# A gated linear attention and a gated MLP on one core: the order of the steps, and the engine of the steps that have a choice, written anew behind the first tenth

## The chip, the core and the metric

The kernel runs on one core of a Trainium2 chip. A core has a tensor engine (PE, with its weight loads shown as PEld), a vector engine (DVE), a scalar engine (ACT), GpSimd (POOL) and SyncE (SP, which here only starts transfers). Each engine works through its own queue of instructions strictly in the order in which the program issued them and waits at semaphores for the others. The metric is the time of one execution on the device, in microseconds.

## The reference

```python
# attention: 4 batches, 8 heads, 768 steps, head dimension 48
mag = sqrt(a_re**2 + a_im**2)
scale = minimum(mag, 0.999) / (mag + 1e-6)
for t in range(768):                      # complex state S, 48 x 48 a head
    S = (a_re + 1j * a_im)[t] * scale[t] * S + k[t] v[t]^T
    y[t] = q[t] @ S.real
x = y, heads side by side                 # 4 x 768 x 384
# gated MLP
h = gelu(x @ w_in);  u, v = halves of h   # 512 columns each
v = layernorm(v) * g_ln
gated = u * (w_sg @ v + b_sg)             # w_sg 768 x 768, over time
out = x + gated @ w_out                   # 512 x 384
```

## The kernel before

The recurrence is done in chunks of 128 steps, 24 chunks in all (g = 0 to 23, 6 a batch). The gates' logarithms are summed along time, and q and k are multiplied by the exponentials of these sums and by the cosines and sines of the summed angles; a chunk is then products of matrices: `pa` (k by q, masked to `am`), `ps` (v by k, the chunk's part of the state S) and `py` (am by v, and S by q), whose result `yp` goes to DRAM and comes back as `x`. The MLP splits every f32 operand into a high and a low part in f32r and makes each product from three matmuls (`mm3`, L230): `pv` and `pu` for x by w_in, `pvs` for w_sg, `po` for w_out. The attention's own matmuls are plain f32.

The work is cut into Python generators, one chain of steps for each piece: `l` load gates, `m` load q and k, `g` logarithms (`logs`), `e` scaling (`scale`), `t`, `p`, `s` angles and their sines, `v` load v, `r` rotate, `z` transposes into heads, `a` a chunk's products (`attend`), `n` the MLP's v half with its layernorm, `x` its u half with the gelu, `y` the spatial product, w_out and the store, `w` splitting of weights, `h` and `k` range checks of gates and weights for a fallback that is not taken, `ok` the verdict on them, `f` constant products. A string, `ORDER`, names the chains one after the other; each name runs the next step of that chain (`:3` three steps), which puts its instructions at the end of their engines' queues. So the string alone sets the order on every engine. Marks behind a name choose the engine of a step that has a choice (`alt`):

- products and differences of two tiles (`ew`): VectorE, or GpSimd with one mark
- copies out of PSUM (`evac`, L205/L207): ScalarE, or VectorE with a mark
- high parts (`high`): ScalarE, GpSimd with one mark, VectorE with two
- masking of `pa` (`causes`): one VectorE operation (L659), or with one mark a ScalarE copy (L656) and a GpSimd product (L657)
- `stoke` (L225): none, one or three constant products of two constant tiles, written to a tile that the next real product overwrites; they only keep the tensor engine at work

`act` puts an ACT_TABLE_LOAD (L193) ahead of a function whose table is not the one loaded last: logarithm and exponential are one table, sine and arctangent another, gelu the third. Other places that the prediction names: L412 `im<-im,inv` in `logs`, L466 `k<-k,em` in `scale`, L522 `left<-csn` in the angles (`turns`), L691 `S<-S,dec` in `attend`, L273 to L279 the first steps of splitting w_out, L871 to L873 the verdict `pok` and `oki`, and L980, where every engine loads the verdict into a register (TENSOR_LOAD) for the branch at the end.

Of the kernel before, what the change touches and what calls it, by code (L numbers as in the profile page):

```python
# [39 lines left out]
e3' e3 n0_0' f z3:3 z3'' p3:2 p3'' p3 f z3:3 f:2 z3 a3:3 f:2 a3 s3:3 w12 e3 a3'' a3:4 n0_0' a3 r4'' r4 w5 w10 t4 p4 v5  # L40
w10:2' w4'' r5'' g4 n0_0:2 z4:6 n0_0:3 z4 r5'' a4 a4'' o0 z4 n0_0:2 g4 l5:2 a4:2 z5:2 w5 a4'' a4 z5' z5:2 m4 z5 g4 m4
z5:2 n0_2 w5 l7 g4 g5 w5 a5 a4:2 a4'' w11 a5' n0_2 a5 a5'' a5' w14 p4:2 e4 n0_0' n0_0'' a4 e4 o1 w11 n0_2'' n0_2 v7
n0_0 p4:2 w11'' p4 s4' a5:2 n0_3 w15 g5:2 e4 e4'' s4:2 r6 e4 r6:2 g5 n0_3 n0_3'' r6 t5 p5 r6'' r6 z6 g5 w15 n0_0'' g5
r6'' z7 n0_0' n0_0'' r6 n0_3'' w5 x0_3 w15 g5 n0_2 g5 n0_3 n0_2 x0_3:2 w15:2 a6 a6' f:10 p5 v6 n0_2 n0_3 x0_3 n0_2''
# [39 lines left out]
def tile_kernel(ctx: ExitStack, tc: tile.TileContext, t_q, t_k, t_re, t_im, u_q, u_k, u_re, u_im, t_v, v, q, k, f_re, f_im,  # L84
# [317 lines left out]

    def logs(n):

        re, im = (part(n, x) for x in ("re", "im"))
        new(n, "inv", "e")
        e = part(n, "inv")
        act(re, re, AF.Ln)
        yield
        act(e, re, AF.Exp, scale=-1.0)  # L410
        yield
        ew().tensor_mul(im, im, e)  # L412
        yield
        new(n, "l")
# [199 lines left out]
    def attend(g):  # L614
# [48 lines left out]
        for g2 in range(early):  # L663
# [390 lines left out]
```

## Time and profile before

| | |
|---|---|
| median of 3 runs | 436.95 us (436.94 to 437.4) |
| profiled execution, span | 434.6 us |
| its own time taken as | the median, 2.35 us above the span |
| PE busy | 421.3 us (97%) |
| DVE busy | 364.5 us (84%), 620 instructions |
| ACT busy | 275.2 us (63%), 378 instructions, 50 of them table loads |
| POOL busy | 150.7 us (35%) |
| longest idle stretches of PE after the start | 1.47, 1.33, 0.89, 0.77 us |

No separate time stands beside the profiled execution, so its span is set against the median. Busy times are sums over an engine's instructions, and matmuls overlap, so PE's 97% says that it is seldom idle, not that it could not be faster. A row of a timeline begins with the start and the duration; in brackets stands how long the engine was idle before it and whose result ended that.

### The profile page before, as it was taken

What the parts mean: (1) busy time and instruction counts of PE and PEld (TensorE: products, weight loads), DVE (VectorE), ACT (ScalarE), POOL (GpSimd) and SP (SyncE); (2) the same over time, 40 slices, a digit from 0 to 9 for tenths busy, and PEclk for the clock granted to TensorE, in tenths of its full rate; (3) what the DMA queues carried; (4) which work ended last, traced back from release to release, by engine and by line L of the source; (5) the groups of instructions that cost most, each with busy time, mean ns of one, the idle gap of its engine ahead of it and who ended that gap; (6) DMA issues with size and microseconds to landing.
All of it is one profiled execution on the core that took longest, in us unless ns stands there. A gap on an engine that the chain in (4) does not pass through costs nothing.

```text
span 434.6 us, 10107 instructions
## 1 busy us (share of the span) xinstructions
PE 421.3 (97%) x3958; PEld 383.6 (88%) x3958; DVE 364.5 (84%) x620; ACT 275.2 (63%) x378; POOL 150.7 (35%) x234
## 2 busy tenths in 40 slices
PE   7999899999999989999999999999999999999994
PEld 6667688788999989889998999989999998899994
DVE  5899899999999999898898999997898776757363
ACT  6999898886999886695666776776750113342010
POOL 7214356203334154446022416532321011326130
PEclk9999999999999999999999999999999999999999
DMA  7577868789478898697959789568947964554531
GB/s 244 176 205 196 268 168 278 223 241 277 149 196 259 243 299 263 208 273 212 271 141 299 217 241 252 168 193 226 320 120 230 330 193 163 187 181 166 157 116 59
DMA packets 78540, 93.54 MB, mean 215 GB/s; under 512 B 10516, under 2 KB 60438, under 8 KB 78488
## 3 DMA queue, kind: packets, MB, share of 16 engines
q1 hardware_dynamic: 78344, 92.65, 71.2%
q8 instruction: 32, 0.52, 0.5%
q10 hardware_dynamic: 144, 0.20, 0.1%
q14 instruction: 20, 0.16, 0.1%
HBM read 69.23 MB, written 23.60 MB: 214 GB/s over the span
## 4 chain that ended last, share of the span: by engine, by line
PE 43%; DVE 29%; issue 8%; POOL 7%; ACT 6%; DMA 4%; SPq 0%; DVEq 0%; POOLq 0%
PE pvs L230 10%; PE pu L230 6%; PE po L822 6%; PE pv L230 4%; PE pa L649 4%; PE py L700 2%; PE pv L225 2%; DVE am L659 2%; PE py L705 2%; DVE tg L838 2%; DVE im L510 2%; PE warm L225 2%; ACT L193 1%; PE ps L675 1%; ACT csn L194 1%
## 5 line engine op out<-in xcount | busy, mean ns | idle before, releaser
L230 PE MATMUL pvs<-wsgh,vh 128*128 128x384 f32 x192 | 65.9, 343 | 0.0
L230 PE MATMUL pvs<-wsgh,vl 128*128 128x384 f32 x192 | 65.3, 340 | 0.2
L193 ACT ACT_TABLE_LOAD x50 | 64.2, 1283 | 1.7 <-PEq L1039 0.9
L230 PE MATMUL pvs<-wsgl,vh 128*128 128x384 f32 x192 | 64.9, 338 | 0.0
L649 PE MATMUL pa<-Q,K 96*64 96x64 f32 (+1 forms) x768 | 41.0, 251 | 1.5 <-DVE am L659 1.5
L649 PEld LDWEIGHTS pa<-Q,K 96*64 96x64 f32 x768 | 36.7, 137 | 6.0 <-ACT ep L194 1.6
L700 PE MATMUL py<-am,vbuf 128*64 128x128 f32 x384 | 39.0, 276 | 2.8 <-DVE am L659 1.7
L230 PEld LDWEIGHTS pvs<-wsgh,vl 128*128 128x128 f32 x192 | 36.1, 188 | 1.4 <-DVE vl L219 0.8
L230 PEld LDWEIGHTS pvs<-wsgh,vh 128*128 128x128 f32 x192 | 36.1, 188 | 0.7 <-issue 0.4
L230 PEld LDWEIGHTS pvs<-wsgl,vh 128*128 128x128 f32 x192 | 36.1, 188 | 0.0
L822 PE MATMUL po<-gh,wouth 128*128 128x384 f32 x96 | 33.0, 344 | 0.8 <-DVE oki L873 0.8
L705 PE MATMUL py<-Q,S 96*48 96x128 f32 x320 | 33.7, 272 | 0.0
L822 PE MATMUL po<-gl,wouth 128*128 128x384 f32 x96 | 32.6, 340 | 0.3 <-DVE gl L219 0.2
L230 PE MATMUL pu<-xh,winh 128*128 128x384 f32 x96 | 32.9, 342 | 0.0
L230 PE MATMUL pu<-xh,winl 128*128 128x384 f32 x96 | 32.3, 337 | 0.0
L822 PE MATMUL po<-gh,woutl 128*128 128x384 f32 x96 | 32.3, 337 | 0.0
L230 PE MATMUL pu<-xl,winh 128*128 128x384 f32 x96 | 32.3, 336 | 0.0
L659 DVE TENSOR_TENSOR am<-pa,masks 128x512 f32<-128x512 f32 x44 | 29.5, 682 | 2.4 <-PE pa L649 2.1
L219 POOL TENSOR_TENSOR gl<-tg,gh 128x384 fp32r<-128x384 f32 x15 | 18.6, 1237 | 34.0 <-DVE gh L216 15.1
L700 PEld LDWEIGHTS py<-am,vbuf 128*64 128x64 f32 x384 | 25.5, 136 | 5.2 <-DVE am L659 3.1
L230 PE MATMUL pv<-winh,xh 128*128 128x512 f32 x72 | 29.4, 408 | 0.0
L194 ACT ACTIVATE vr<-pv 128x512 f32<-128x512 f32 x24 | 14.3, 599 | 22.7 <-PE pv L230 13.7
(286 smaller groups left out, 1125.2 us busy)
## 6 DMA issues: line engine op xcount, KB each, us to landing
vbuf<-in_t_v_dram SPq DMA_DIRECT2D x24, 288.0 KB, 3.9
K<-rk SPq DMA_DIRECT2D x18, 384.0 KB, 4.4
Q<-rq SPq DMA_DIRECT2D x18, 384.0 KB, 6.8
x<-xd SPq DMA_DIRECT2D x9, 576.0 KB, 5.6
xd<-yp SPq DMA_DIRECT2D x48, 96.0 KB, 3.5
gr<-in_f_im_dram SPq DMA_DIRECT2D x12, 384.0 KB, 5.3
gr<-in_f_re_dram SPq DMA_DIRECT2D x12, 384.0 KB, 3.9
out_dram<-x SPq DMA_DIRECT2D x23, 192.0 KB, 3.5
```

The lines of the kernel that those rows point to most:

```text
L193: nc.scalar.preload_act_table_set(SETS[t])
L194: nc.scalar.activation(out, in_, func, scale=scale, **kw)
L219: ew().tensor_tensor(out=l, in0=src, in1=h.bitcast(F32), op=ALU.subtract)
L225: nc.tensor.matmul(o, mask[:, 0:n], u_turn[:, 0:o.shape[1]], start=True, stop=True, skip_group_check=True)
L230: nc.tensor.matmul(o, w(i), x(i), start=(i == 0 and j == 0), stop=(i == n - 1 and j == 2))
L510: nc.vector.tensor_tensor_scan(out=im[:, kt, :], data0=im[:, kt, :], data1=im[:, kt, :], initial=run["left", b, c0][:, kt:kt + 1] if c0 el ...
L649: nc.tensor.matmul(pa[rows, hh, j:], K(h)[:, j:j + KB], Q(h)[:, j:], start=True, stop=True)
L659: nc.vector.tensor_tensor(out=pairs(am), in0=pairs(pa), in1=causal, op=ALU.mult)
L700: nc.tensor.matmul(py[64 * e:64 * e + 64, p_, :], Vy(h)[:, 0:64], ams[h // 4][:, h % 4, :], start=True, stop=c == 0)
L705: nc.tensor.matmul(py[64 * e:64 * e + D, p_, :], Sb[:, h, :], Q(h), start=False, stop=True)
L822: nc.tensor.matmul(po[d], w[:, f, ds], g[:, f, :], start=f == 0 and j == 0, stop=f == NF - 1 and j == 2)
L838: ew().tensor_mul(tg, us[f], tg)
```

## The change

The first three lines of `ORDER` stay (up to some 30 us of the run). Everything behind them is written anew: which step comes when, and the marks. Operations and buffers are the same. Three code edits only let a step fetch a tile later than before, so that steps can stand in another order.

```diff
 ORDER = """
 ...
-s1:2 a0 e1 w3 t2 w6' w6 r1:2'' l3:2 g2:5 e0 w3:2 o1 v1 p2 z1 z1'' w3 w3' z1 z1' m2:2 e2:2 p2' e2 g3 p2 a0 w4 g3:2 w3'
+s1:2 a0 e1 w3 t2 w6' w6 r1'' g2 r1'' g2 l3 e0 l3 w1'' g2 o0 p2 g2 p2' g2 w3:2 z1 v1 z1 w3 z1 g3 e1 p2 e2:2 f p2 z1' m2
 ...
-y3_0:2'' y3_0' y3_3 h22:2 x3_0 k5 k7:2 y3_0:2 k5 ok:2 y3_0 x3_0 y3_0:2 y3_0' y3_0'' y3_0:10
+y3_0:2 k0 h10 h21 y3_0'' y3_0' y3_0 f x3_0 y3_0 k0 h21 k8 x3_0 y3_0 y3_0'' y3_0' y3_0:8 y3_0' y3_0 k8 y3_3 ok y3_0:7
+ok y3_0
...
     def logs(n):
-        re, im = (part(n, x) for x in ("re", "im"))
+        re = part(n, "re")
...
+        im = part(n, "im")
         ew().tensor_mul(im, im, e)
...
     def scale(n):
-        q_, k_ = (U[n][x] for x in ("q", "k"))
...
-            ew().tensor_mul(at(k_, i), at(k_, i), at(em, i))
+            k_ = at(U[n]["k"], i)
+            ew().tensor_mul(k_, k_, at(em, i))
...
-            ew().tensor_mul(at(q_, i), at(q_, i), at(ep, i))
+            q_ = at(U[n]["q"], i)
+            ew().tensor_mul(q_, q_, at(ep, i))
...
-        Sb = run.get(("S", g - 1))
+        Sb = lambda: run["S", g - 1]
```

The lines of the kernel after are those of before plus 6 to 8. What changes in number, over the whole program: constant products 40 to 37. ACT: 373 to 402 instructions in the path that runs; table loads 50 to 65, `kt` copies 11 to 20, `yp` copies 11 to 14, `gh` casts 9 to 12, copies of `pa` 4 to 1. DVE: 620 to 595; `kt` copies 19 to 10, `yp` copies 13 to 10, S times dec 12 to 6, `vl` 19 to 15, `am` 44 to 47, `im` by inv 7 to 10. POOL: 239 to 247; S times dec 4 to 10, `vl` 5 to 9, `em` from k and csn 0 to 4, `am` 4 to 1, `im` by inv 4 to 1. On PE, the places where plain f32 and f32r matmuls follow each other with no transpose between them: f32 then f32r 15 to 11, f32r then f32 9 to 5; with transposes between them 35 to 25. Table loads that stand between the matmuls of 80 and of 220 us of the run before: 24 to 32.

Three places, with the order of one engine before and after.

PE at the end of the program, in the last `po` products. `po` is one tile of the result, `pok` the verdict of the range checks. Before:

```order
L822 MATMUL po_5308<-gh_5187,wouth_124 128x384
L822 MATMUL po_5308<-gl_5193,wouth_124 128x384
L822 MATMUL po_5308<-gh_5187,woutl_125 128x384
L871 MATMUL pok_5333<-ones_5331,ok1_5319 1x2
L980 TENSOR_LOAD oki_5335
L822 MATMUL po_5351<-gh_5187,wouth_124 128x384
L822 MATMUL po_5351<-gl_5193,wouth_124 128x384
```

After:

```order
L830 MATMUL po_5318<-gh_5225,woutl_125 128x384
L879 MATMUL pok_5372<-ones_5370,ok1_5358 1x2
L830 MATMUL po_5328<-gh_5225,wouth_124 128x384
L830 MATMUL po_5328<-gl_5228,wouth_124 128x384
L830 MATMUL po_5328<-gh_5225,woutl_125 128x384
L830 MATMUL po_5338<-gh_5225,wouth_124 128x384
L830 MATMUL po_5338<-gl_5228,wouth_124 128x384
L830 MATMUL po_5338<-gh_5225,woutl_125 128x384
L988 TENSOR_LOAD oki_5374
```

The load of the verdict has moved from in front of the `po` products to behind the last of them.

DVE around the small copy `left` of the angles that before runs at 158 us; `am` is a masked `pa`, for which `py` waits. Before:

```order
L688 TENSOR_TENSOR S<-ps,S 96x384
L838 TENSOR_TENSOR tg<-u__1764,tg 128x384
L659 TENSOR_TENSOR am<-pa_114,masks 128x512
L522 COPY left<-csn_2059 128x3
L659 TENSOR_TENSOR am<-pa_1397,masks 128x512
L205 COPY dec<-pd 96x16
```

After:

```order
L526 SCALAR_TENSOR_TENSOR csn_2066<-csn_2066,im_1387 128x768
L530 COPY left<-csn_2066 128x3
L419 TENSOR_TENSOR im_1928<-im_1928,inv_2001 128x768
L696 TENSOR_TENSOR S<-ps,S 96x384
L473 TENSOR_TENSOR k_2064<-k_2064,em_2094 128x768
L211 COPY kt<-pk 128x384
L559 TENSOR_SCALAR csn_2066<-csn_2066 128x768
L667 TENSOR_TENSOR am<-pa_114,masks 128x512
```

The copy stood directly ahead of an `am`; now five other operations stand between them, and the product k by em next to it has come from POOL to DVE.

ACT in the logarithms and gelus that before run from 120.9 to 132 us (`l`, `im`, `re`, `inv` are gates, `u` a gelu). Before:

```order
L193 ACT_TABLE_LOAD
L194 ACTIVATE l_1607<-l_1607,cols 128x768
L207 COPY yp<-py 128x512
L193 ACT_TABLE_LOAD
L194 ACTIVATE im_1502<-im_1502 128x768
L194 ACTIVATE gh<-tg 128x384
L193 ACT_TABLE_LOAD
L194 ACTIVATE re_1069<-re_1069 128x768
L194 ACTIVATE gh<-tg 128x384
L194 ACTIVATE inv_1504<-l_1607,cols 128x768
L193 ACT_TABLE_LOAD
L194 ACTIVATE u__1751<-pu 128x384
```

After:

```order
L199 ACT_TABLE_LOAD
L200 ACTIVATE u__1632<-pu 128x384
L200 ACTIVATE gh<-tg 128x384
L199 ACT_TABLE_LOAD
L200 ACTIVATE l_1616<-l_1616,cols 128x768
L199 ACT_TABLE_LOAD
L200 ACTIVATE im_1402<-im_1402 128x768
L200 ACTIVATE gh<-tg 128x384 x2
L199 ACT_TABLE_LOAD
L200 ACTIVATE inv_1409<-l_1616,cols 128x768
L199 ACT_TABLE_LOAD
L200 ACTIVATE u__1749<-pu 128x384
```

A gelu now stands alone between two gate functions, which makes five table loads of four.

## Rows read from the trace of the kernel before

**Rows 1.** The page: busy time, share of the span and instructions of each engine, and the granted clock of the tensor engine in 40 equal slices, in tenths.

```profile
PE 421.3 (97%) x3958; PEld 383.6 (88%) x3958; DVE 364.5 (84%) x620; ACT 275.2 (63%) x378; POOL 150.7 (35%) x234
...
PEclk9999999999999999999999999999999999999999
```

**Rows 2.** Busy time of each engine in five stretches of the run: length, then PE, PEld, DVE, ACT and POOL with their instructions, the granted clock of PE, the share of the DMA engines and GB/s.

```profile
30.00:80.00 50.00, 47.21 (x581) 37.51 (x580) 46.61 (x74) 44.53 (x68) 25.69 (x34) 1.00 0.77 231
80.00:160.00 80.00, 79.14 (x831) 74.27 (x825) 77.38 (x119) 70.15 (x90) 24.98 (x37) 1.00 0.80 233
160.00:220.00 60.00, 59.40 (x628) 54.70 (x629) 53.39 (x89) 42.40 (x56) 24.49 (x32) 1.00 0.81 237
220.00:330.00 110.00, 109.73 (x1107) 104.63 (x1103) 99.46 (x158) 71.84 (x91) 36.48 (x44) 1.00 0.77 226
330.00:434.60 104.60, 98.27 (x669) 93.38 (x667) 64.92 (x142) 21.03 (x39) 26.50 (x38) 1.00 0.55 174
```

**Rows 3.** What PE waited for, over the whole run: total in us, times, longest.

```profile
PE py L700 <- DVE am L659: 1.7, 2, 1.3
PE pa L649 <- DVE am L659: 1.5, 1, 1.5
PE py L700 <- POOL am L657: 0.9, 1, 0.9
PE po L822 <- DVE oki L873: 0.8, 1, 0.8
```

**Rows 4.** Timeline of PE in short stretches: start, duration, operation, idle before it.

```profile
52.72 0.74 PE L649 MATMUL pa<-Q,K 96*64 96x128 f32 x12 [1.47 <-DVE am L659]
...
66.65 0.48 PE L230 MATMUL pv<-winh,xh 128*128 128x512 f32 x1
66.97 0.39 PE L230 MATMUL pv<-winl,xh 128*128 128x512 f32 x1
...
83.74 8.80 PE L225 MATMUL pv<-u_turn,masks 128*128 128x256 f32 x40
...
105.87 0.39 PE L230 MATMUL pv<-winl,xh 128*128 128x512 f32 x1
106.10 0.40 PE L230 MATMUL pv<-winh,xl 128*128 128x512 f32 x1
106.43 0.78 PE L649 MATMUL pa<-Q,K 96*64 96x128 f32 x13
...
160.60 0.44 PE L700 MATMUL py<-am,vbuf 128*64 128x128 f32 x4 [1.33 <-DVE am L659]
...
161.09 0.39 PE L700 MATMUL py<-am,vbuf 128*64 128x128 f32 x4
161.31 0.39 PE L705 MATMUL py<-Q,S 96*48 96x128 f32 x4
161.63 0.44 PE L230 MATMUL pu<-xh,winh 128*128 128x384 f32 x1
161.91 0.34 PE L230 MATMUL pu<-xl,winh 128*128 128x384 f32 x1
162.09 0.34 PE L230 MATMUL pu<-xh,winl 128*128 128x384 f32 x1
...
424.44 0.41 PE L822 MATMUL po<-gh,wouth 128*128 128x384 f32 x1 [0.77 <-DVE oki L873]
```

**Rows 5.** Timeline of DVE at the stalls of 51 and 159 us.

```profile
48.33 0.36 DVE L273 TENSOR_SCALAR bits<-raw 128x384 int32<-128x384 int32 x1 [1.92 <-DMA raw<-in_moe_w_out_dram]
...
51.89 0.68 DVE L659 TENSOR_TENSOR am<-pa,masks 128x512 f32<-128x512 f32 x1
...
157.99 1.97 DVE L522 COPY left<-csn 128x3 f32<-128x3 f32 x1
159.87 0.68 DVE L659 TENSOR_TENSOR am<-pa,masks 128x512 f32<-128x512 f32 x1
```

**Rows 6.** Timeline of POOL at the stalls of 78 and 159 us.

```profile
77.92 1.27 POOL L657 TENSOR_TENSOR am<-am,masks 128x512 f32<-128x512 f32 x1
...
158.11 1.82 POOL L466 TENSOR_TENSOR k<-k,em 128x768 f32<-128x768 f32 x1
```

**Rows 7.** The tile `left`: durations in ns (minimum, median, maximum), first and last start.

```profile
L522 DVE COPY left<-csn x6: 154/164/2639, 84.2 to 263.0; 128x3 f32<-128x3 f32 x6
```

**Rows 8.** Timeline of ACT: a function (sine), a table load and the next function (logarithm).

```profile
144.80 0.85 ACT L194 ACTIVATE im<-im 128x768 f32<-128x768 f32 x1
145.66 1.28 ACT L193 ACT_TABLE_LOAD   x1
146.95 0.94 ACT L194 ACTIVATE l<-l,cols 128x768 f32<-128x768 f32 x1
```

**Rows 9.** Groups of instructions by line and shape: count, busy time, mean ns of one, idle before.

```profile
L193 ACT ACT_TABLE_LOAD x50 | 64.2, 1283 | 1.7 <-PEq L1039 0.9
...
L207 ACT COPY kt<-pk 128x384 f32<-128x384 f32 x11 | 5.2, 469 | 1.2 <-PE pk L631 1.2
...
L205 DVE COPY kt<-pk 128x384 f32<-128x384 f32 x19 | 10.2, 547 | 0.4 <-PE pk L631 0.2
...
L691 DVE TENSOR_TENSOR S<-S,dec 96x384 f32<-96x384 f32 x12 | 7.1, 592 | 0.3
...
L691 POOL TENSOR_TENSOR S<-S,dec 96x384 f32<-96x384 f32 x4 | 4.9, 1234 | 9.8 <-DVE S L688 9.8
```

More of the change, by code (lines that the diff above doesn't have):

```diff
@@ L40 @@
[L40 to L44, printed above, removed]
@@ new lines @@
+z1 a0 w4 w3' e2 g3 z1 m2 z1 w3' w7 a0 p2 g3 p2' f a0 z1' p2 e2' l4 a1 w1' a1'' e2 w4 e2 g3 a1 e2 g3 e2' f e2 a1 p2 w4
+a0 e2 a1'' t3 w7' s2 f a0 s2 a1 v2 w7'' l4 g3 w4 a1 s2 w9 g3 f g3 e2 r3 r2 g4 g3:2 p3 r2 r3 a1 z3 w12 g3 z3' e3 w2''
+w9' w12 w4' p3 z2:2 e3 w12 z2 w9 a1 z2:3 z3 z2 e3 a2 z2 v3 w12 m3 e3' g4 a2'' e3 p3 g4 a2 m3 e2 a2 z3 e3 z3 a2:2 w4''
+a2'' p3 w12 e3 a1 p3 g4 z3 e3'' w12' w8 e3 l7 w8 e3 n0_0 p3'' p3 g4 z3 a3 z3 a2 a3 a2 w5 g4 s3 a3:2 w8' n0_0' a3'' a3
+n0_0 a2 s3 a3:2 s3 w5 t4 n0_0 r4'' n0_0 a3 r5'' e3 r4 z4 p4 z4 n0_0:2 r5'' n0_0 l5 z4:3 w10 v4 z4:3 n0_0 a4 a4'' a4
@@ new lines @@
+w10:2' e3 l5 a4 g4 z5:2 w5:2 a4'' z5:2 a4 z5 g4 a3 v5 g5 n0_0 m4 z5 g4 z5 n0_2 w11 a4' z5 a5 g5 a4 x0_0 a5 p4 n0_2 a5
+a5'' n0_0' p4 a4 m4 a4 n0_2' w11 w11'' e4 p4:2 w14 a5 e4:2 a5 n0_2 p4 s4' s4 e4'' s4 g5 n0_0'' r6 g5 w5' a5 n0_0 n0_3
+w15 r6:3 e4 r6'' t5 g5 n0_3 v6 w5 n0_0'' g5 f r6 z6 n0_0 g5 n0_3'' r6'' z7 n0_3'' w15 p5 w15:2 n0_2 p5 r6 x0_3 n0_2
+w15 x0_3 p5 w15' z6 x0_3 p5 w14:2 f w14 p5 x0_3 l6 n0_2 x0_3 w14 n0_0'' n0_3 a6 w14 o1 n0_2 n0_2' z7 a6 n0_3 a6 a7' a7
+n0_3 n0_2' m5 v7 n0_3 l7 n0_3:2 l6 x0_3 a6 n0_3 g6 a6 x0_3 a7 e4 x0_0 g5 n0_3 s5 a7'' e4'' g6 m5 p5 a6 n0_3 a6 n0_3''
@@ new lines @@
+a6 n0_3' a6 n0_3' g5 a6 a7 n0_3'' n0_3' a6 n0_3' a6 a7'' a6' e5 a7 a7'' a7 n0_3'' e5'' a7 o1 n0_3 n0_3'' g6'' s5:2 a7'
+e5 a7 y0_3 g6 r8 y0_3 v9 a6 v8 e5 r8 g7 x0_3 y0_3:2 r8'' r8 e5 r8'' r8 y0_3' y0_3 r8 g6 y0_3 t6 y0_3' x0_0'' y0_3
+y0_3' y0_3:2 y0_3'' g6 p6 z8 y0_3 a7' g6 z9 y0_3:2 r8 y0_3 x0_0:2 l8 x0_0 p6 g6 x0_0 y0_3 a8 z8 m6 a9 a8:3 y0_3'' x0_0
+z9 m6 p6 y0_3:2 a9'' g6 p6:2 y0_3 a9 f s6'' a8 a8'' g7 a8:2 e6 a8 a9' s6 e6' g7 a8 e5 e5' y0_3 a7 a8' a8 s6 r10 a9 l8
+e6 v10 g7 a9 r10 a9 r10'' y0_3 e6'' a8' y0_3 e6 g7 r10 x0_0 a8 y0_0 y0_3 r10'' t7 g8 g7 y0_0 y0_3 p7 y0_0 p7 y0_0 y0_3
@@ new lines @@
+g7 a9 y0_0:2 p7 r10 g7:2 z10 r10' r10 y0_0 m7 p7 g8 x0_0 y0_0' a10:2 z10 l9 p7 e7 p7 g8 a10 a9 y0_0' a9 y0_3 m7 a9'
+e7:2 z11 e6 a10' a9 z11 n1_0 a10 a9 f s7' s7 e7' s7 y0_0' a10 r12 e6 a10 y0_0 a10'' x0_0 a10:2 a11 a9 r12 g8 r12' r12
+y0_0 a10 e7 g8 y0_0'' r12 v11 a10 r12 n1_0 a10 g8 y0_0 y0_0' g8 n1_0 f a11'' a11 z12 g8 t8 r12' y0_0 n1_0 l9 f a10
+a11'' e7 y0_0 a11 a12 g9:2 p8 r12 p8 z13 y0_0' p8 z12 n1_0 y0_0'' a11'' n1_0 a11 a12:3 p8 g9 m8 n1_0 p8 v12 n1_0:2 g8
+y0_0' n1_0:2 y0_0 g9:2 n1_0 y0_0 n1_3 y0_0 n1_0 y0_0 e8 e8'' p8 l10 e8 f y0_0 a12 m8 s8:2 a12'' n1_0' g9 n1_3:2'' s8
@@ new lines @@
+a12 n1_0'' n1_0' r14 e7'' n1_0'' a12'' z13 a12 a13 t9 l10 n1_0'' y0_0 r14 n1_0 y0_0 n1_3 r14:2 v13 n1_3 n1_0' n1_3
+n1_0 n1_3 a12 n1_3:2 n1_0' n1_3:2 a13 e8' x1_3 a13 n1_3 e8 a13 f g10 z14 a13 m9 a12 p9 g9 p9 a13 n1_3 a12' a13 a13''
+x1_3 a13 z15 a13 r14'' y0_0 a13'' p9 r14 e8 r14 a12 n1_3' a13 f n1_3 r14 a14' n1_3'' a14 n1_3'' v14 n1_3:2' n1_3'' g9
+x1_3:2 a13 n1_3:2 x1_3:2 g9 p9 y1_3:2 p9 y0_0 y1_3 l11 z14 x1_3 y1_3'' g10 e9 z15 y1_3 g10 s9 y1_3 e8' a15 y1_3 s9 a14
+y1_3' s9 a15 a14 g10 e9'' a15 a14:3 r16' a13 m9 v15 a14'' t10 a14:2 x1_0 y1_3' e9 r16 y1_3 a15 r16'' e9'' f p10 a14'
@@ new lines @@
+r18 y1_0' y1_0:2 x1_0 p11 y1_0 p11 y1_0' n2_0 g12 y1_0 e11 y1_0 n2_0 y1_0 a16 a17 n2_0 y1_0 y1_0'' p11 k2 n2_0 p11 v19
+y1_0 v18 n2_0:2 a18 a17 n2_0 g12 n2_3 a19' a18' n2_0 h9 n2_0:2 z18 y1_0 z19 s11 a19'' y1_0 n2_0 y1_0 e11 y1_0 s11 n2_0
+y1_0:2 s11 n2_0 y1_0 a18 y1_0 a18' h9 m11 h1 n2_0' a19 r20' h16 a18 p12 a18:3 e10:2 n2_0'' a18 a19 f a19 g12 y1_0
+a18:2 p12 n2_0 n2_3'' a19'' a19 k2 a19 r20 a18 n2_3 r20 e11 a18 e11'' a19:2 a19' n2_0 a19 n2_3:2 n2_0'' n2_3 h22 n2_0'
+n2_3 r20 z20 g12 n2_3:2 n2_0'' n2_3 e11 r20'' x2_3 a19 n2_3:3 v21 n2_3 x2_3:2 z21 x2_3 n2_3' x2_3 h1 x2_0 p12 n2_3''
@@ new lines @@
+n2_3' a20 a21 a20 x2_3 n2_3 r20 h16 m12 n2_3'' a20 v20 r20'' x2_3 n2_3'' n2_3 n2_3'' g12 x2_0 p12 x2_0'' k3 r20 y2_3:2
+p12 a21 a20 x2_3 y2_3 y2_3'' k12 e12 y2_3' y2_3 k9 x2_0 k3 y2_3:2 k12 s12 k9 k1 x2_0 h22 f s12 z21 e12 y2_3'' s12
+y2_3' x2_0 r22' x2_0 y2_3:2 y2_0 y2_3 y2_0 e12 y2_3'' y2_3' z20 h20 y2_3 k1 m12 h17 x2_0 r22 a21 y2_3 a20:2 r22' a20
+y2_3'' x2_0 a20 r22 a19 e11 e12' a20 z22 a21 h11 e11'' e12 a20 a21 a20'' a20 a21'' h20 h11 a21 r22 y2_3'' h6 a21
+y2_3'' r22 a20' a21:2 e12 a21' a21 a22' r22 a22:2 r22 h3 a20 y2_3:2 y2_0' z23 y2_3 z22 y2_3 f z23 y2_3:2 v22 y2_3:2 h3
@@ new lines @@
+y2_0' e12'' x2_0 h6' y2_0'' y2_0:2 y2_0'' a22' y2_0:3 a22:2 a21 a22 h17 y2_3 a22:2 h14 a22 a21 v23 y2_0 a22' x2_0
+y2_0' a23 a22 a23 a22 a23 a23'' y2_0 n3_0 a23 a22 a23' y2_0' h5 n3_0' h2 y2_0 n3_0 h14 a23 n3_0:2 h5 h15 y2_0 n3_3 h2'
+n3_0 y2_0 y2_0'' n3_0:4 y2_0 h15 n3_0 h8 n3_0 n3_3 y2_0 k7 k6 h7 y2_0:2 n3_0 y2_0 n3_0' n3_3 n3_0'' n3_0' k6 h12 n3_3
+h8 n3_0' y2_0 n3_3 n3_0'' n3_0 n3_3:2 k7 n3_3:2 n3_0:2' n3_3 n3_0 x3_3 y2_0 n3_3 y2_0 x3_3 h12 k4 n3_3:2 y2_0 n3_3'
+n3_3'' x3_3 n3_3 n3_3' x3_3 n3_3' k4 x3_3 n3_3' k11 x3_3 y2_0 h0 h7 n3_3' h4 n3_3'' x3_3 n3_3 y3_3:2 k11 y3_3'' k5
@@ L687, in attend @@
             else:
-                nc.vector.tensor_tensor(out=Sn, in0=ps[0:2 * D], in1=Sb, op=ALU.add)
+                nc.vector.tensor_tensor(out=Sn, in0=ps[0:2 * D], in1=Sb(), op=ALU.add)
                 yield
@@ L704, in attend @@
                     h = 2 * p_ + e
-                    nc.tensor.matmul(py[64 * e:64 * e + D, p_, :], Sb[:, h, :], Q(h),
+                    nc.tensor.matmul(py[64 * e:64 * e + D, p_, :], Sb()[:, h, :], Q(h),
                                      start=False, stop=True)
```

44 lines of the change are left out of this document (7 added, 37 removed).

## The prediction

> **What bounds the kernel now.** First the page: PE is busy 97% of the span and DVE, the next, 84%, while the granted clock stands at its higher level (2.4 GHz) in all forty slices [rows 1]. Whatever shortens the run must therefore take work off PE or close one of its few idle stretches; work on another engine counts only through these. Second, the table of five stretches, because an average over the run hides the tight places. From 30 to 80 us PE loses 2.79 of 50 us; DVE is busy for 46.61 of these (93%) and ACT for 44.53 (89%). From 80 to 160 us DVE is at 97% and ACT at 88%, and PE loses 0.86 of 80. From 160 to 220 ACT falls to 71% and PE loses 0.60, from 220 to 330 it loses 0.27 of 110 [rows 2]. Third, the waits of PE: nearly all are for `am` (1.7, 1.5 and 0.9 us) and for the verdict of the range checks (0.8) [rows 3]. Fourth, the timeline of PE at these waits gives each its place: 1.47 us before 52.72, 1.33 before 160.60, 0.77 before 424.44 [rows 4], and the 0.9 us for POOL's `am` [rows 3] end when it is there at 79.19 [rows 6].
>
> The profiled span is 434.6 us and the median 436.95. I take the 2.35 us between them as unchanged, sum on the span and add them at the end.
>
> **The change part by part.** Operations are the same, so there are six places where time can come or go.
>
> *The end of PE.* Today PE loads the verdict into its register in the middle of the `po` products and idles 0.77 us for it [rows 4]. Behind the change this load stands after the last `po`, where nothing on PE follows but the branch. The two transfers on SP now stand ahead of SP's own load, the additions of `x` on DVE ahead of DVE's; the last transfer, on ACT, stands behind ACT's load, but the verdict's matmul comes six matmuls before the end, so it should be there. I take -0.77, with -0.77 and 0 as ends.
>
> *The stall at 159 us.* DVE's copy `left`, 128 x 3, took 1.97 us [rows 5], against a median of 0.164 [rows 7]. It ran while POOL multiplied k by em from 158.11 to 159.93 [rows 6], and ended 0.03 us behind that product. `am` stood next in DVE's queue and started at 159.87; PE idled 1.33 us for it. In the new order that product is on DVE itself and five operations lie between the copy and the next `am`. I take -1.33; if another POOL operation of two operands falls on a copy with an `am` behind it, this is 0. By the Trainium skill, "SBUF — State Buffer", section "Who interferes with whom", VectorE and GpSimd share a pair of ports that one instruction can hold for its whole length, so that the other is blocked and not slowed. The 1.97 against 0.164 us agree with it. By that rule the change's six more S times dec and four more `vl` and `em` each on POOL speak against it, since they hold the ports more often; no row says how many of them would fall on something that PE waits for.
>
> *The stalls at 51 and 78 us.* In the first, DVE had waited 1.92 us for a piece of w_out [rows 5], and `am` came out late behind the work piled up. In the new order the first operation on w_out still stands only four operations ahead of an `am`. I take 0, with -1.47 as the other end. In the second, `am` went through ACT and POOL, and POOL's half alone took 1.27 us [rows 6] where DVE's whole one takes 0.68 [rows 5]. Three of the four `am` of this kind become DVE's. But DVE is 93% busy there, and what the path through POOL costs in length it saves in queueing. I take 0, with -0.9 as the other end.
>
> *Plain f32 beside f32r on PE.* From a `py` group to the first `pu`, 0.32 us pass where 0.22 is the pitch of such groups (161.09, 161.31, 161.63), and from the first `pu` to the next 0.28, where 0.18 follows [rows 4]. So a return from f32 costs some 0.10 + 0.10 = 0.20 us. In the other direction 106.10 to 106.43 is 0.33, where the interval before was 0.23: 0.10 us. Before, 15 x 0.20 + 9 x 0.10 = 3.9; after, 11 x 0.20 + 5 x 0.10 = 2.7. I take -1.2. Where transposes lie between, 66.65 to 66.97 is 0.32, not 0.23, so a return is 0.09 dearer there; there are ten fewer changes of this kind, five of them returns: 0 to -0.45, and I take 0, since the first transposes may pay it anyway.
>
> *Three constant products fewer.* Twenty steps took 8.80 us on PE, so one is 0.44 [rows 4] and three are 1.3. Two of the three stood before `pk` and one before `py` of the early chunks, in the first stretch of the table, where PE has idle time anyway and DVE is busiest but for the next [rows 2]. I take half, -0.6, with -1.3 and 0 as ends. That the clock would miss them is a rival, below.
>
> *The load moved between engines.* DVE loses work: nine `kt` copies at 0.547 and six S times dec at 0.592 are 8.5 us of its 364.5, and the rest of its changes about cancel. POOL takes the six at 1.234, 7.4 us, and has room (35%). ACT takes nine `kt` copies at 0.469 = 4.2, and above all 15 more table loads at 1.283 = 19.2 us [rows 9]. ACT has 160 us free over the run, but nearly all behind 220 us. Between 80 and 220 us lie eight more loads, 10.3 us, and with the copies perhaps 15 us of new work; ACT is busy for 70.15 + 42.40 = 112.6 of 140 us there (80%) and would come to 127 (91%). That is above the 89% of the stretch from 30 to 80, in which PE loses 5.6%, and above the 88% of the stretch from 80 to 160, in which it loses 1.1% [rows 2]. Which of the two it will resemble depends on DVE, which stays where it is or gets a little lighter in both. One row speaks for 1.1% and one for 5.6%. PE's present loss in these 140 us is 1.46. At 1.1% it would be 1.5, at 5.6% 7.8. So the cost is 0 to 6.3 us, and I take 1.9, a third of the way, because the row with DVE at 97% is the nearer in time and in kind.
>
> *Sum.* -0.77 - 1.33 - 1.2 - 0.6 + 1.9 = -2.0. The span becomes 432.6 and the time 432.6 + 2.35 = 435.0 us.
>
> **The rivals.**
>
> *A: ACT becomes the second bound from 80 to 220 us (slower).* The mechanism is one: an isolated gelu between two gate functions makes two table loads, ACT's queue runs late, and with it everything behind it in program order: `kt` copies (which hold `ps` and so S and `py`), exponentials em and ep (which hold k, q and the transposes). PE then waits where today it waits for nobody. For it speaks that the new order has five loads in the place of four within a dozen instructions, and ACT's 91%. Against it, that today only one wait of any size comes from ACT's side (by way of POOL's `am`, 0.9) [rows 3]. Price: +6.3 us at the loss of the first stretch; with the other gains, of which the stall at 159 us is already counted in the 1.46, -0.77 - 1.2 - 0.6 = -2.6, the span is 438.3 and the time 440.7. It decides from about half that price: at +3.2 the time is 437.6. In the trace a load takes 1.28 us and the next function starts 0.01 us later [rows 8]. The Trainium skill, "ScalarE: Activation LUTs", section "Step-by-step: what each stage is for", puts a change of table at about 2.7 us with the drain; the rows show no such drain, so the measured 1.28 decides. By the page's figure the 15 loads would be 40 us and this rival nearly sure.
>
> *B: the waits come back elsewhere (no change).* The new order closes two stalls and opens as many of the same kind, the constant products only become idle time, and ACT costs its 1.9: -0.77 - 1.2 + 1.9 = -0.1, so 434.5 and 436.9. For it: about 4 us of such stalls inside a run at 97% look like what a dense order leaves, and DVE stays at 93 to 97% up to 160 us [rows 2].
>
> *C: everything closes (faster still).* ACT costs nothing, and the stalls at 51 and 78 us go too: -0.77 - 1.33 - 1.2 - 1.3 - 0.45 - 1.47 - 0.9 = -7.4 at most, and about -5 with half of the last five terms: 429.6 and 432.
>
> *D: the clock falls.* With fewer constant products PE could be granted the lower level (1.2 GHz) for a while. Today the clock holds through idle stretches of 1.47 us [rows 1, 4], and after the change PE has as much work as before, so I hold this for nearly excluded.
>
> **How the numbers follow.** A measurement of this kernel tells about 0.2%, 0.9 us, from no change, so "same" is 436.1 to 437.8. The forecast (434.0 to 436.0) has 0.45, A 0.24 (437.8 to 441), B 0.18, C 0.11 (430 to 434), D 0.02. Faster: 0.45 + 0.11 and a little of B's edge, 0.57. Same: 0.18, from B and the lighter half of A's edge. Slower: 0.25. The range leaves out half of C and the upper part of A: 432.0 to 440.0.
>
> **What would show it.** In the profile after: no idle time of PE at the end for the verdict; no copy `left` of 2 us with `am` right behind it; PE's busy time lower by 1 to 2.5 us; 65 table loads, some 83 us of ACT; the stretch from 80 to 220 with ACT near 90% and PE's loss not above 3.5 us. The prediction is wrong if PE's waits have ACT's copies and exponentials in them with over 3 us in total (A), if the sum of PE's waits is as it was (B), or if the granted clock leaves its higher level (D).

## The result, and the profile after

| | before | after |
|---|---|---|
| median | 436.12 us (434.87 to 438.08, 19 runs) | 438.65 us (436.99 to 442.19, 19 runs) |
| after : before | | 1.007, interval 1.0049 to 1.009 |
| span of the profiled execution | 434.6 us | 436.5 us |

The change makes the kernel slower by 0.7% (the medians lie 2.5 us apart), where I had forecast 435.0 us and faster. The page of the kernel after, to be held against [rows 1]:

```profile
span 436.5 us, 10115 instructions
## 1 busy us (share of the span) xinstructions
PE 419.2 (96%) x3952; PEld 382.7 (88%) x3952; DVE 357.2 (82%) x596; ACT 297.6 (68%) x406; POOL 169.7 (39%) x242
```

PE has 2.1 us less work, as forecast, and the run is longer: PE waits more. Its waits, to be held against [rows 3] (total, times, longest):

```profile
PE pa L657 <- DVE am L667: 2.9, 2, 2.3
...
PE py L708 <- DVE am L667: 1.2, 2, 0.9
PE pv L236 <- DVE xl L225: 1.1, 2, 0.7
PE pa L657 <- ACT Q L213: 0.8, 1, 0.8
PE phi L539 <- ACT im L200: 0.7, 1, 0.7
PE pk L639 <- DMA K<-rk: 0.6, 1, 0.6
PE pvs L236 <- POOL vl L225: 0.5, 1, 0.5
```

The wait for the verdict is gone and the number of waits has grown, but one stands out, 2.3 us for an `am`. The five stretches (busy time of PE, PEld, DVE, ACT, POOL, then the granted clock), to be held against [rows 2]:

```profile
30.00:80.00 50.00, 46.28 (x580) 37.02 (x580) 48.58 (x73) 44.87 (x71) 28.82 (x28) 1.00 0.77 229
80.00:160.00 80.00, 78.72 (x788) 74.06 (x783) 76.33 (x117) 70.70 (x89) 33.16 (x40) 1.00 0.79 235
160.00:220.00 60.00, 57.66 (x579) 52.25 (x578) 53.71 (x81) 52.31 (x69) 26.05 (x34) 1.00 0.83 238
220.00:330.00 110.00, 108.46 (x1097) 103.54 (x1094) 89.67 (x148) 82.23 (x105) 39.65 (x47) 1.00 0.77 226
```

PE's loss grows by 0.93, 0.42, 1.74 and 1.27 us. From 80 to 220 us ACT is busy for 123.0 of 140 us (88%, against 80%), near the 91% of my estimate, so this looks like rival A. And PE's waits for ACT (`Q`, `im` and two smaller ones) come to 2.1 us, where before has none of 0.2 us or more. The timelines at the two places that cost most say something else. First PE itself:

```profile
61.88 0.89 PE L657 MATMUL pa<-Q,K 96*64 96x128 f32 x16 [2.27 <-DVE am L667]
...
165.15 0.89 PE L657 MATMUL pa<-Q,K 96*64 96x128 f32 x16 [0.62 <-DVE am L667]
...
167.84 0.44 PE L708 MATMUL py<-am,vbuf 128*64 128x128 f32 x4 [0.92 <-DVE am L667]
```

Then DVE (start, duration) ahead of these waits:

```profile
57.44 0.54 DVE L473 TENSOR_TENSOR k<-k,em 128x384 f32<-128x384 f32 x1
57.91 2.16 DVE L478 TENSOR_TENSOR q<-q,ep 128x384 f32<-128x384 f32 x1
...
61.04 0.68 DVE L667 TENSOR_TENSOR am<-pa,masks 128x512 f32<-128x512 f32 x1
...
161.02 3.48 DVE L559 TENSOR_SCALAR csn<-csn 128x768 int32<-128x768 int32 x1
164.42 0.68 DVE L667 TENSOR_TENSOR am<-pa,masks 128x512 f32<-128x512 f32 x1
```

and POOL at the same times:

```profile
56.73 2.92 POOL L225 TENSOR_TENSOR wsgl<-raw,wsgh 128x768 fp32r<-128x768 f32 x1 [1.76 <-ACT wsgh L200]
...
159.84 1.47 POOL L699 TENSOR_TENSOR S<-S,dec 96x384 f32<-96x384 f32 x1 [0.18 <-DVE S L696]
161.28 1.84 POOL L478 TENSOR_TENSOR q<-q,ep 128x768 f32<-128x768 f32 x1
163.09 0.99 POOL L225 TENSOR_TENSOR gl<-tg,gh 128x384 fp32r<-128x384 f32 x1
```

The product `q<-q,ep` takes 2.16 us, where its equal in size just ahead took 0.54; it ends 0.4 us behind POOL's low part of w_sg. The copy `csn` (L559, the sign cleared ahead of the sines) takes 3.48 us; the median of its six is 0.546. It overlaps three operations of POOL that follow one another and ends 0.4 us behind the last. `am` stands behind both in DVE's queue. The mechanism looks like that of the stall at 159 us before [rows 5 to 7], which the change removed; this profile shows two others.

### The profile page after: what moved, and what is told of

It reads as the page before. It is cut to its first block, busy times and chain, and to the rows that moved or that the text cites. A ratio compares the mean times of both kernels' runs of the same rounds, so it can differ in the third digit from the quotient of the medians.

```text
span 436.5 us, 10115 instructions
## 1 busy us (share of the span) xinstructions
PE 419.2 (96%) x3952; PEld 382.7 (88%) x3952; DVE 357.2 (82%) x596; ACT 297.6 (68%) x406; POOL 169.7 (39%) x242
## 4 chain that ended last, share of the span: by engine, by line
PE 39%; DVE 8%; DMA 5%; ACT 3%; issue 2%; POOL 2%; SPq 2%; DVEq 0%; POOLq 0%; ACTq 0%
PE pvs L236 12%; PE po L830 7%; PE pv L236 7%; PE pu L236 6%; PE pa L657 3%; DMA xd<-yp 2%; DMA Q<-rq 2%; PE ps L683 2%; PE py L708 1%; DMA K<-rk 1%; DVE csn L559 1%; SPq L596 1%; PE py L713 1%; DVE lo L449 1%; ACT L199 1%
## 5 line engine op out<-in xcount | busy, mean ns | idle before, releaser
L199 ACT ACT_TABLE_LOAD x65 | 83.4, 1283 | 1.9 <-PEq L1047 0.9
L657 PE MATMUL pa<-Q,K 96*64 96x128 f32 (+1 forms) x768 | 40.8, 250 | 4.2 <-DVE am L667 2.9
L667 DVE TENSOR_TENSOR am<-pa,masks 128x512 f32<-128x512 f32 x47 | 31.9, 683 | 7.0 <-PE pa L657 6.7
L225 POOL TENSOR_TENSOR gl<-tg,gh 128x384 fp32r<-128x384 f32 x15 | 17.7, 1179 | 39.1 <-DVE gh L222 23.2
L236 PE MATMUL pv<-winh,xl 128*128 128x512 f32 x72 | 28.7, 398 | 1.2 <-DVE xl L225 1.1
```

Source lines behind the costliest of these rows:

```text
L199: nc.scalar.preload_act_table_set(SETS[t])
L225: ew().tensor_tensor(out=l, in0=src, in1=h.bitcast(F32), op=ALU.subtract)
L236: nc.tensor.matmul(o, w(i), x(i), start=(i == 0 and j == 0), stop=(i == n - 1 and j == 2))
L657: nc.tensor.matmul(pa[rows, hh, j:], K(h)[:, j:j + KB], Q(h)[:, j:], start=True, stop=True)
L667: nc.vector.tensor_tensor(out=pairs(am), in0=pairs(pa), in1=causal, op=ALU.mult)
```

## The experiments

Two theories. **Ports:** the loss comes from operations of VectorE held beside GpSimd just ahead of what PE waits for. **ACT:** it comes from 15 more table loads. Names such as `s7'` in the diffs are entries of `ORDER`; each ratio is to the kernel before, with its interval.

**No table loads.** `before_oneset` and `after_oneset` leave gelu, sine and arctangent out:

```diff
     def act(out, in_, func, bias=None, scale=1.0, **kw):
+        if table["on"] and table_of.get(func, 0):
+            func = AF.Identity
```

> The kernel before, with gelu, sine and arctangent replaced by the identity (these values are left out of the result), so that one table serves the whole run and 49 of 50 table loads go. Theory ACT (the change loses by its 15 more table loads): PE waits little for ACT today, so 0.993 to 0.998 of before. Theory ports (it loses where VectorE is held up beside GpSimd): 0.997 to 1.000.

> The kernel after with the same identity in place of gelu, sine and arctangent, so that 64 of 65 table loads go. Theory ACT: with the loads gone the shorter work of PE shows, 1.5 to 2.5 us below the same kernel made from before. Theory ports: it stays at least 1.5 us above that one.

Measured: 1.0055 (1.0035 to 1.0074) from before, 1.0097 (1.0062 to 1.0132) from after. Without its table loads after is not faster than before without them, so theory ACT, which wanted 1.5 to 2.5 us less, falls. (Part of the 0.4% between them is clock, below: 4 of the 6 executions of the second.) In its profile PE's waits for ACT have shrunk to 0.2 us and others stand in their place, 1.9 us for an `am` and 1.4 us for POOL's `vl` among them. Nor did ports foresee that before would become slower by 0.55% with ACT 64 us lighter. One new stall, in the timeline of DVE without loads:

```profile
134.83 3.37 DVE L444 TENSOR_TENSOR_SCAN lo<-going,lo 128x384 f32<-128x384 f32 x2
138.13 0.53 DVE L207 COPY kt<-pk 128x384 f32<-128x384 f32 x1
138.57 1.27 DVE L661 TENSOR_TENSOR am<-pa,masks 128x512 f32<-128x512 f32 x2
```

```profile
135.00 2.38 POOL L414 TENSOR_TENSOR im<-im,inv 128x768 f32<-128x768 f32 x1 [3.40 <-ACT inv L196]
```

The same two scans and the same product in before:

```profile
134.92 1.80 DVE L442 TENSOR_TENSOR_SCAN lo<-going,lo 128x384 f32<-128x384 f32 x2
```

```profile
136.26 2.10 POOL L412 TENSOR_TENSOR im<-im,inv 128x768 f32<-128x768 f32 x1 [4.57 <-ACT inv L194]
```

The scans take 3.37 us, not 1.80, while POOL has the product, which ACT released 1.3 us earlier than in before; PE waits 1.38 us for `am`. In this profile a lighter ACT moved work of POOL onto work of DVE.

**The two held operations**, first both, then one at a time:

```diff
-f s7' s7 e7' s7 y0_0'
+f s7:2 e7' s7 y0_0'
...
-a3:2 w8' n0_0' a3'' a3
+a3:2 w8 n0_0' a3'' a3
```

> The kernel after with two steps moved to other engines: the copy with the sign cleared ahead of the sines at 161 us from VectorE to ScalarE, and one low part of w_sg at 57 us from GpSimd to VectorE. Theory ports: the waits of PE of 0.62, 0.92 and 0.57 us from 164 to 178 go and that of 2.27 at 60 us shrinks to about 1.6, so 2 to 3 us less than after, 0.999 to 1.002 of before. Theory ACT: ScalarE gets 0.84 us more, so as after, 1.005 to 1.009.

> The kernel after with only the copy with the sign cleared (161 us) moved from VectorE to ScalarE. Theory ports: PE's waits of 0.62 and 0.92 us behind the held copy go, and the later load of K behind them, 1.5 to 2.1 us less than after, 1.002 to 1.004 of before. Rival (the gain of the two edits came from shifts all along the run): as after, 1.006 or more.

> The kernel after with only the one low part of w_sg (57 us) moved from GpSimd to VectorE. Theory ports: the wait of 2.27 us shrinks and part of it comes back 2 us later because VectorE has 0.95 us more to do, 0.7 us less than after, 1.004 to 1.007 of before. Rival: 1.007 or more.

Measured: both 0.9991 (0.9963 to 1.0019), `s7` alone 1.0043 (1.002 to 1.0066), `w8` alone 1.002 (0.9992 to 1.0048). From 1.007, that is 0.8%, 0.3% and 0.5%. With both, the loss of the change is gone; `w8` alone takes most of it; the 0.3% of `s7` lies within the two intervals, so it is not shown by itself. In `w8` alone the product of q by ep is short again (DVE's timeline):

```profile
56.50 0.55 DVE L477 TENSOR_TENSOR q<-q,ep 128x384 f32<-128x384 f32 x1
```

This repeats: in all four profiles that leave the low part of w_sg on GpSimd at that place (after, after without table loads, `s7` alone, and the kernel with S times dec on VectorE, below) the product takes 2.16 to 2.18 us, and in all six that move it in after's order 0.54 or 0.55.

The copy `csn` at 161 us does not repeat. In `w8` alone it is where after has it, with the same operations of POOL around it (DVE, then POOL):

```profile
158.98 0.71 DVE L558 TENSOR_SCALAR csn<-csn 128x768 int32<-128x768 int32 x1
```

```profile
159.24 2.17 POOL L477 TENSOR_TENSOR q<-q,ep 128x768 f32<-128x768 f32 x1
```

Here the copy ran through between two operations of POOL, and POOL's second took 2.17 us, not 1.84; PE waits for no `am` there, only 0.60 us for the transfer of Q. In after without table loads the same copy takes 0.72 us. So 3.48 us is what one execution shows, and the share of this copy in the loss stays open.

`w8` gave 2.2 us where I expected 0.7. Its wait of 2.27 us became one of 1.10 (the work now ahead of the next `am`), and the waits behind the copy were absent from its profile; the clock, below, may have a part.

**The same mechanism in before:** the stall mended, and the copy of the signs put on VectorE.

```diff
-s7 e7' p7 g8 a10 a10''
+s7 e7' g8 a10 a10'' p7
...
-a5'
+a5
```

> The kernel before with the small copy left at 158 us put behind the masked product that PE waits for, and with the masked product of 78 us made by one VectorE operation in place of ScalarE and GpSimd. If a stall of PE counts with its full width, 1.33 and up to 0.9 us go, 0.995 to 0.998 of before. Rival: what stands behind comes no earlier (transfers, other waits), 0.999 to 1.001.

```diff
-s7 e7' p7
+s7' e7' p7
```

> The kernel before with the copy with the sign cleared of the same angles moved the other way, from ScalarE to VectorE, where GpSimd's product of k by em runs beside it at 158 us. Theory ports: it is held until that product ends, and the masked product behind it comes later by 0.5 to 1.5 us, 1.001 to 1.004 of before. Rival: ScalarE has 0.84 us less to do and nothing is lost, 0.998 to 1.000.

Measured: 0.9985 (0.9964 to 1.0006) and 1.0019 (1.0000 to 1.0039). In the second the copy is held as expected:

```profile
158.92 2.36 DVE L551 TENSOR_SCALAR csn<-csn 128x768 int32<-128x768 int32 x1
161.20 0.16 DVE L522 COPY left<-csn 128x3 f32<-128x3 f32 x1
161.27 0.68 DVE L659 TENSOR_TENSOR am<-pa,masks 128x512 f32<-128x512 f32 x1
```

It ends at 161.28, 0.4 us behind a product k by em on POOL (159.05 to 160.86), and PE waits 1.81 us there. In the first, the wait at 159 us is gone from the profile, and at 78 us PE now waits 1.49 us for another `am`: a mended wait is worth less than its width.

**The end.** In before, the verdict placed as in after:

```diff
-ok:2
...
-y3_0:10
+y3_0:2 ok y3_0:7 ok y3_0
```

> The kernel before with the verdict of the range checks taken after the first of the last three results and loaded at the very end, as after has it. By the term of the prediction 0.77 us less, 0.998. Rival: the end is set by the additions and the store behind it, and nothing is gained, 1.000.

Measured: 1.0002 (0.9983 to 1.0022). PE's last matmul ends at 428.76 us, not 429.38, but the span is 434.8, not 434.6. The transfers of the last microseconds, KB and us from issue to landing, of before and then of this kernel:

```profile
out_dram<-x ACTq DMA_DIRECT2D x1, 192.0 KB, 3.0
```

```profile
out_dram<-x ACTq DMA_DIRECT2D x1, 192.0 KB, 3.8
```

The last store is issued 0.62 us earlier and lands 0.8 us slower; the two on SP ahead of it are slower too (3.0 us, not 2.2). Over the profiles of all kernels here, the time from PE's last matmul to the end of the span is 5.1 to 5.4 us in the seven with the early verdict, 5.5 to 6.1 in the thirteen with the late one (5.44 and 5.45 where they come nearest). Why the stores land slower stays open.

**Less work for GpSimd in general:**

```diff
-                ew().tensor_tensor(out=Sn, in0=Sn, in1=by, op=ALU.mult)
+                nc.vector.tensor_tensor(out=Sn, in0=Sn, in1=by, op=ALU.mult)
```

> The kernel after with all ten products S times dec on VectorE, none on GpSimd (before has four there). If it is GpSimd's use of the port in general, VectorE is held less and the run is 1 to 3 us shorter than after, 1.000 to 1.005 of before. If only the few places count where a held operation stands ahead of what PE waits for, VectorE's 5.9 us more are about as dear as what they save, 1.005 to 1.009.

Measured: 1.0076 (1.0054 to 1.0098), as after. At 57 us the product q by ep is held as in after (2.17 us), and PE waits 2.28 us. At 161 us the copy `csn` has no operation of POOL beside it and takes 0.55 us, but PE waits there all the same, for a transfer (DVE, then PE):

```profile
164.86 0.55 DVE L558 TENSOR_SCALAR csn<-csn 128x768 int32<-128x768 int32 x1
```

```profile
163.00 1.56 PE L656 MATMUL pa<-Q,K 96*64 96x128 f32 x32 [1.45 <-DMA Q<-rq]
```

So ten operations fewer on GpSimd left the hold at 57 us, and the time, as they were. This profile shows the clock. PE behind the wait at 60 us in after and then here, 62 to 66 us:

```profile
62.00:66.00 4.00, 4.00 (x54) 3.42 (x54) 3.77 (x7) 3.95 (x6) 0.00 (x0) 1.00 0.57 171
```

```profile
62.00:66.00 4.00, 4.00 (x48) 3.88 (x45) 3.42 (x7) 3.97 (x5) 0.00 (x0) 0.57 0.55 180
```

Behind a wait of the same length the granted clock stayed at its higher level in one execution and averaged 0.57 in the other, mostly at the lower level (1.2 GHz). Among all executions 8 of 19 of after have a mean granted clock under 0.995, 6 of 12 with `s7` mended, 8 of 11 here; with `w8` mended 1 of 12, and of before, as timed beside the experiments, 2 of 138. So the wait at 57 to 62 us comes with a lower clock in nearly half of the executions. It is not the only place that can: with the copy of the signs on VectorE in before (PE waits of 2.0 and 1.8 us) it is 4 of 12. What the fall costs is not settled by the record: in after the medians of the executions at 0.995 or more and of those below lie 0.5% and 0.8% above before, with `s7` mended 0.1% and 0.7%.

**More places mended, and orders joined.** After with `s7`, `w8` behind both `am`, and the low part of v at 117 us on VectorE; then two orders that join before and after and have this last edit too.

```diff
-f s7' s7 e7' s7 y0_0'
+f s7:2 e7' s7 y0_0'
...
-a3:2 w8' n0_0' a3'' a3 n0_0 a2 s3 a3:2
+a3:2 n0_0' a3'' a3 n0_0 a2 s3 a3 w8 a3
...
-n0_3'
+n0_3
```

> The kernel after with the copy with the sign cleared (161 us) on ScalarE, the low part of w_sg (57 us) on VectorE behind both masked products that PE waits for there, and the low part of v that PE waits for at 117 us on VectorE. Theory ports: all three of the waits behind held operations go (2.27, 0.62, 0.92, 0.55 us and the K load of 0.57), 4 to 4.9 us less than after, 0.995 to 0.999 of before. Rival: the waits come back at the next tight place, 1.000 to 1.003.

> The order of before up to some 65 us (372 steps), then the remaining steps in the order of after, with the sign copy at 161 us on ScalarE and the low part of v at 117 us on VectorE. Theory ports (the place at 57 us is avoided, the others are mended): idle time of PE about 1.5 us less than before and its work about 1 us less, the end 0.5 us longer, 0.994 to 0.998. Rival: the junction or other waits cost as much, 1.000 or more.

> The order of after with the three steps mended up to some 165 us (760 steps), then the remaining steps in the order of before, whose PE hardly waits there and which keeps its early verdict. Sum of the waits seen so far: about 2 us less idle time and 1.5 us less work than before, 0.991 to 0.996. Rival: the junction or other waits cost as much, 1.000 or more.

Measured: 1.0123 (1.0084 to 1.0162), 1.009 (1.0054 to 1.0125), 1.0177 (1.0144 to 1.0209), all slower. The edit at 117 us made a wait of its own (DVE, then PE, of the first):

```profile
111.72 0.69 DVE L224 TENSOR_TENSOR vl<-vr,vh 128x512 fp32r<-128x512 f32 x1 [2.23 <-POOL vh L219]
112.33 0.68 DVE L666 TENSOR_TENSOR am<-pa,masks 128x512 f32<-128x512 f32 x1
```

```profile
113.07 0.69 PE L707 MATMUL py<-am,vbuf 128*64 128x128 f32 x4 [2.39 <-DVE am L666]
```

```profile
113.00:117.00 4.00, 3.93 (x34) 3.60 (x35) 4.00 (x8) 3.94 (x5) 1.38 (x1) 0.57 0.00 0
```

VectorE's queue stands for 2.23 us for the high part, which GpSimd still makes, with `am` behind it; the clock falls behind the wait in the profiles of all three. Without this edit:

> The kernel after with the sign copy (161 us) on ScalarE and the low part of w_sg (57 us) on VectorE, behind both masked products that PE waits for there; the low part of v at 117 us stays where after has it. If the two held operations and the 1.1 us that the first form of the edit left are the loss: 0.995 to 0.999 of before, and the clock stays up. If there is more of the same elsewhere: 1.000 to 1.004.

> The order of before for 372 steps (some 65 us), then that of after, with only the sign copy moved to ScalarE; no new wait of VectorE for GpSimd's high part of v. Ports: without that 2.4 us wait and the fall of the clock behind it, 0.996 to 1.000. Rival: the later stretches of after are dearer than those of before whatever happens at 57 and 161 us, 1.003 or more.

Measured: 0.9985 (0.9962 to 1.0008) and 0.9994 (0.9963 to 1.0025), no execution under 0.995 in clock. The low part of v alone thus costs 1.4% (1.0123 against 0.9985), more than the wait of 2.4 us and the clock behind it; but the profile of the first shows the fastest of its six executions. That rest, and a wait of 3.07 us at 176 us in the third (for an `am` whose queue waited for ACT), were not followed up.

The first of the two kernels without the edit at 117 us also shows why the mended change brings no gain. In its profile PE has 2.4 us less work than in before (418.9 us, not 421.3) and as much more idle time, in waits of 1.0 us and less for VectorE, ACT and transfers.

**The constant products**, left out of before (without and with the copy `left` moved), and put back into after:

```diff
-z1'
+z1
...
-z5'
+z5
...
-a5'
+a5
```

> The kernel before without the three constant products that after leaves out (37 in place of 40), nothing else. By the term of the prediction 0.6 us less (0 to 1.3): 0.997 to 1.000. Rival: the clock falls more often without them, 1.001 or more.

> The same with 37 constant products, and the small copy left at 158 us behind the masked product that PE waits for. By the terms 0.6 and 1.33 us less: 0.994 to 0.998. Rival: the wait comes back later, 0.998 to 1.001.

> After with the same two edits (sign copy, low part of w_sg) and the three constant products put back at their steps, 40 in all. If they are run in time that PE would wait anyway, as without them before did not get faster: 0.997 to 1.000. If they cost their 1.3 us here: 1.000 to 1.003.

Measured: 1.0024 (1.0002 to 1.0046), 1.0002 (0.9973 to 1.0031), and 0.9964 (0.9944 to 0.9984). In before they cost nothing: without them PE comes earlier to the `am` of 78 us and waits longer there, 1.54 us where it was 0.9 [rows 3].

```profile
79.11 0.44 PE L700 MATMUL py<-am,vbuf 128*64 128x128 f32 x4 [1.54 <-POOL am L657]
```

With them in after's mended order, PE's own work to its last matmul is 1.5 us longer than without, and its idle time 2.7 us shorter, in one profile of each. This last kernel is faster than before and after, by an interval that ends at 0.9984; from the same order with 37 constant products (0.9985) it is not told apart. Its page:

```profile
span 433.8 us, 10126 instructions
## 1 busy us (share of the span) xinstructions
PE 420.4 (97%) x3958; PEld 384.3 (89%) x3958; DVE 353.1 (81%) x596; ACT 298.3 (69%) x407; POOL 164.8 (38%) x241
```

One more wait, the `am` of 58 us put ahead of two operations on the angles:

```diff
-p3'' p3 g4 z3 a3 z3 a2 a3
+g4 z3 a3 z3 a2 a3 p3'' p3
```

> As the run before last of after with two edits (sign copy on ScalarE, low part of w_sg behind the masked products), and the masked product of 58 us ahead of the two VectorE operations on the angles that stood before it. If a wait of 0.65 us counts with its width: 0.995 to 0.998 of before, under both kernels. Rival: it comes back within the next 10 us, 0.998 to 1.000.

Measured: 0.9987 (0.997 to 1.0005), against 0.9985 without it: the 0.65 us wait is gone and one of 0.47 stands at 61 us, so it came back, as the rival has it.

## Why the prediction was wrong

- *What bounds the kernel* was right: PE's waits decided.
- *The end of PE*, -0.77: the wait went, the time did not (1.0002 when done alone). The term counted PE's last matmul as the end, but the last store ends the run, and it landed later behind PE's last matmul.
- *The stall at 159 us*, -1.33: gone as forecast. **The step that failed is here.** The term took the held copy as a thing to be removed, with 0 as its worst end, and no term of the sum gave a price to the new order's VectorE operations beside GpSimd. The runs show that price: a product at 57 us, held to 2.16 us, makes PE wait 2.27 us, and moving GpSimd's operation away takes 0.5% (2.2 us) off the time; with the copy at 161 us moved as well it is 0.8%, some 3.4 us, the whole loss. The copy itself stood in the order shown ahead of the prediction (L559 ahead of `am`), but it was held 3.48 us in one profile only. The Trainium skill, "SBUF — State Buffer", section "Who interferes with whom", says that VectorE's copies and operations with scalars can contend with GpSimd for the shared ports, and that its operations of two SBUF operands contend with GpSimd instructions that read SBUF. The trace agrees with 2.16 us against 0.54, and in one execution a copy was held through three GpSimd operations in a row. The prediction quoted this section against the change and did not look for its places, though both queues follow from `ORDER`.
- *The stalls at 51 and 78 us*, 0, with only a gain as the other end: the second went. The first was 1.47 us in before and 0.79 in after, but in three more profiles with before's order up to there it is 0.55, 1.06 and 2.01 us, so no change is shown. The 2.27 us at 60 us is new and lies between the two.
- *f32 beside f32r* and *constant products*, -1.2 and -0.6: PE's work from start to last matmul, idle time left out, fell from 421.3 to 419.2 us, 2.1 us for a forecast 1.8 in span. But less work ahead of a place where PE waits is not a saving: without the three constant products before took 1.0024. What the fewer switches save was not run by itself, and the work varies from profile to profile (420.9 and 419.2 us in the two of before with 37 constant products).
- *Load moved to ACT*, +1.9: ACT's busy time came as worked out (83.4 us of table loads), and PE's waits for ACT, 2.1 us, are near the 1.9. But the loads did not carry the loss: without them after stayed behind before, and with the two edits, which leave all 65 in place, the loss is gone. The measured time lies in the range of rival A, by another mechanism.
- *Rival D*, the clock, held for nearly excluded because it stayed up behind 1.47 us: it falls behind waits of 2.27 to 2.4 us in part of the executions. The 2.27 us wait was new, so no row of before could show it.

Shown by runs: with the two edits the loss is gone, and GpSimd's low part of w_sg at 57 us carries most of it. Open: the share of the copy at 161 us, and how much is the width of the wait and how much the clock. The forecast gain of 2 us did not come even then (0.9985 to 0.9991, and 0.9964 with the constant products put back): in the profiles PE's smaller work came back as idle time.

## What to carry to other kernels

When an order is changed, lay the queues of VectorE and GpSimd side by side, and look at each operation that stands ahead of what the bounding engine waits for: GpSimd's operations of two operands beside it made one four times as long in all four profiles that have the two side by side, and another six times as long in one profile. Moving the one step to another engine repaired it; moving ten other operations off GpSimd did not. Look at a second execution, or at another kernel with the same step, before a held operation is blamed. Busy shares did not tell this: the engine whose share grew most, ACT, did not carry the loss, and taking its load away made before slower; in that profile the shift brought a new pair together.

## What was not expected of the hardware

- A VectorE copy of 0.55 us held to 3.48 us through three GpSimd operations without a gap between them, in one execution; in two other kernels with the same operations around it, it took 0.71 and 0.72 us.
- Behind a PE wait of 2.27 to 2.4 us the granted clock averaged 0.55 to 0.60 over the next 4 us in four profiles and 1.00 in two. The length alone does not decide: in the kernel with S times dec on VectorE it also fell some 2 us after a wait of 1.45 us, and in the order of after that goes over to before's at 165 us it stayed up behind 3.07 us.
- The last store landed in 3.8 us, not 3.0, and the two before it in 3.0, not 2.2, in the kernel that loads its registers for the branch at the very end; one profile of each, cause open.
